# Projecting queries and keys in 64-row pairs, with the maxima steps spread one to a tile

## The chip, the cores and the metric

The kernel runs on one NeuronCore of a Trainium2 chip. The metric is the device time of one execution in microseconds (us): the median of several runs. A profiled execution gives the trace, from which single rows are read. The engines are PE (TensorE: matmuls, with PEld its weight loads), ACT (ScalarE), DVE (VectorE), POOL (GpSimd) and SP (SyncE, which here issues most DMAs).

## The reference

The result mixes an attention block and a Fourier block by a gate per row, for 2048 rows of width 640:

```
x = A_x                                    # (1, 2048, 640)
g = sigmoid((x * gate_w).sum(-1))
qkv = x @ wqkv                             # 32 heads of 20
p = softmax(q @ k.T * 20 ** -0.5)
a = (p @ v).reshape(1, 2048, 640) @ wo
b = Cr @ (x @ Wre.T) - Ci @ (x @ Wim.T)    # Cr, Ci: 2048 x 2048
out = g * a + (1 - g) * b
```

Inputs and output are float32. The weights wqkv and wo are large (scaled by 64), so the scores are large too and the softmax needs the maximum of every row.

## The kernel before

**Numbers as two parts.** A float32 factor is kept as two parts of the type fp32r: its rounded value and the rest. A product of two such factors takes three matmuls: first by first, first by second, second by first (`three`, L117 to L120). `split` (L110) makes the two parts: a copy by one engine (L112 or L114) and a subtraction by another (L115).

**Stages.** All instructions are put in order by hand, in program order for each engine; semaphores do the rest.

1. Load x and the first weights; project the queries and keys of the first column blocks and all values (up to about 107 us in the profile). `qk_tile(c, t)` (L301) projects column block `c` (128 columns of the queries or keys) for row block `t` (512 rows): 5 blocks of the inner dimension x 3 products = 15 matmuls of 128 x 128 weights on 512 columns, into one PSUM bank.
2. The stretch that the change touches, from about 107 to 256 us: the loop over `order` (eight column blocks, four row blocks each, 32 tiles) projects the rest of the queries and keys. Three things take turns on PE in it:
   - a projected tile, with `hid_done` above 0: ACT copies the bank to SBUF (L319), POOL splits the copy into two parts (L114 and L115), and SP stores both to DRAM (`stores`, `flush`, L299);
   - a feature tile (`hid_tile`, L352), the first step of the Fourier block. Its 15 products are issued as pairs: the 128 inner rows are cut into halves of 64 rows, and the two halves go into two banks of their own, `yp0` and `yp1` (L362). ACT copies one bank (L370), DVE adds the other (L371), SP stores the sum;
   - a maxima step (`s_step`, L188): for two heads, a matmul of 60 rows on 512 columns each (L170) into a bank, and for each bank a DVE maximum along its 512 columns (L172). The two heads lie in partitions 0 to 59 and 64 to 123. These are the row maxima that the attention needs; `LEAD` = 41 steps are to be done before the attention begins.
3. From about 256 us on: attention, with the remaining feature tiles and the sequence transform filled into PE's queue after a written pattern (`ORDER`), and at the end the output projection.

**Segments.** Ahead of every third projected tile (`m % 3 == 0`), ten times (`HEAD`), stands `segment` (L377). By `FILL[4] = (0, 8, 7, 0)` it issues four maxima steps in this order: step, step, 8 pairs of the feature tile, step, 7 pairs, step. A projected tile holds no step. One last step follows after the loop (`run_s(LEAD)`).

**Banks.** `bank()` (L124) hands out five PSUM banks in turn, `ps0` to `ps4`, to every user alike: projected tiles, maxima steps (two banks each), the transpose of the maxima (L204, once in this stretch, after step 33). Whoever gets a bank waits until its last reader is done. Three more banks are `av`, `yp0` and `yp1`.

**Other work in the stretch.** After the second tile of a column block the loaded weights are split by ACT and DVE: once the wide weights of a feature stage (L112 and L115, tile `wb`), otherwise 128 x 640 of the next column block (tile `part`).

Of the kernel before, what the change touches and what calls it, by code (L numbers as in the profile page):

```python
# [11 lines left out]
R = mybir.dt.float32r  # L12
AF = mybir.ActivationFunctionType
ALU = mybir.AluOpType
# [9 lines left out]
ND = D // P  # L24
# [15 lines left out]
LEAD = 41  # L40


FILL = {4: (0, 8, 7, 0)}
HEAD = 10


# [23 lines left out]
def f32(ap):  # L70
    return ap.bitcast(F32)
# [3 lines left out]
def mix_kernel(ctx: ExitStack, tc: tile.TileContext, xa, wqk, wb, cdft, wo, out):  # L75
    nc = tc.nc
    pe, act, dve, pool, sp = nc.tensor, nc.scalar, nc.vector, nc.gpsimd, nc.sync
# [32 lines left out]
    def split(dst1, dst2, src, e1, e2):  # L110
        if e1 is act:
            act.activation(dst1, src, AF.Copy)  # L112
        else:
            e1.tensor_copy(dst1, src)  # L114
        e2.tensor_tensor(dst2, src, f32(dst1), op=ALU.subtract)  # L115

    def three(ps, st1, st2, mv1, mv2, first, last):  # L117
        pe.matmul(ps, st1, mv1, start=first, stop=False)  # L118
        pe.matmul(ps, st1, mv2, start=False, stop=False)  # L119
        pe.matmul(ps, st2, mv1, start=False, stop=last)  # L120
# [3 lines left out]
    def bank():  # L124
        return ps_w.tile([P, 512], F32, name=f"ps{next(turn) % 5}")

    def pair_tile():
        return work.tile([P, 2, 512], F32, name="p", bufs=5)

    def raw_tile():  # L130
        return work.tile([P, 1024], F32, name="raw", bufs=3)
# [56 lines left out]
    def s_step(i):  # L188
        for fn in [s_mm(i, h) for h in range(2)]:
            fn()  # L190
        s_end(i)
# [4 lines left out]
    def new_y(z):  # L196
        yp[z] = ps_y.tile([P, 512], F32, name=f"yp{z}")
        return yp[z]
# [26 lines left out]
    def block(z, t):  # L225
        return proj.tile([P, ND * 512], R, name=f"x{z}{t}")

    xs = [[block(z, t).rearrange("p (d c) -> p d c", d=ND) for t in range(4)] for z in range(2)]
# [32 lines left out]
    def idle(n):  # L261
        ps = bank()
        for _ in range(n):
            pe.matmul(ps, zeros[:, :P], zeros, start=True, stop=True)

    wt = {}

    def load_wqk(c):
        raw = raw_tile()[:, : ND * P].rearrange("p (d c) -> p d c", d=ND)
        sp.dma_start(raw, wqk[c])  # L270

        def finish():
            w = part_tile().rearrange("p z c -> p (z c)")[:, : 2 * ND * P].rearrange("p (z d c) -> p z d c", z=2, d=ND)
            split(w[:, 0], w[:, 1], raw, act, dve)
            wt[c] = w

        return finish
# [17 lines left out]
    stores, halves, hid_done = [], [], 0  # L295

    def flush(keep=0):
        while len(stores) > keep:
            sp.dma_start(*stores.pop(0))  # L299

    def qk_tile(c, t):  # L301
        w = wt[c]
        ps = bank()
        x1, x2 = xs[0][t], xs[1][t]
        for d in range(ND):
            if (c, t) == (0, 0) and d > 0:
                if d == 1:
                    idle(3)
                pe.matmul(ps, w[:, 0, d], x1[:, d], start=False, stop=False)
                pe.matmul(ps, w[:, 1, d], x1[:, d], start=False, stop=False)  # L310
                pe.matmul(ps, w[:, 0, d], x2[:, d], start=False, stop=d == ND - 1)
            else:
                three(ps, w[:, 0, d], w[:, 1, d], x1[:, d], x2[:, d], d == 0, d == ND - 1)
        if hid_done:
            if not halves:
                raw = pair_tile()
                halves.extend((raw[:, 1], raw[:, 0]))
            raw = halves.pop()
            act.activation(raw, ps, AF.Copy)  # L319
        st = pair_tile()  # L320
        st1, st2 = st[:, 0].bitcast(R), st[:, 1].bitcast(R)
        if hid_done:
            split(st1, st2, raw, pool, pool)
        else:
            split(st1, st2, ps, act, dve)
        stores.append((qk_scr[:, t, c * P : (c + 1) * P].rearrange("z p c -> p z c"), st))
        flush(1 if hid_done else 2)

    def mm_b(j, s, ps, n):
        w = wt["b", j]  # L330
# [21 lines left out]
    def hid_tile(i, read_out):  # L352
        j, st = divmod(i, NS)
        hf, ri = divmod(j, 2)
        new_y(0), new_y(1)
        w = wt["b", 2 + j]
        t, cs = st // 4, slice(st % 4 * P, (st % 4 + 1) * P)
        for d in range(ND):
            for z, (xz, wz) in enumerate(((0, 0), (0, 1), (1, 0))):
                for h in range(2):  # L360
                    r = slice(64 * h, 64 * h + 64)
                    pe.matmul(yp[h][:, :HE], xs[xz][t][r, d, cs], w[r, wz, d, :HE],  # L362
                              start=d == 0 and z == 0, stop=d == ND - 1 and z == 2)
                if (d, z) != (ND - 1, 2):
                    yield
        a = raw_tile()[:, :HE]
        y0, y1 = yp[0][:, :HE], yp[1][:, :HE]

        def read():
            act.activation(a, y0, AF.Copy, scale=-1.0 if ri else 1.0)  # L370
            dve.tensor_tensor(a, a, y1, op=ALU.subtract if ri else ALU.add)  # L371

        read_out(read, (a_scr[ri, hf, st], a))
        yield


    def segment(i, steps):  # L377
        def read_out(read, args):
            read()
            stores.append(args)  # L380

        tile_ = hid_tile(i, read_out)
        for n in FILL[steps]:
            run_s(step + 1)
            for _ in range(n):
                next(tile_)

    step = 0

    def run_s(upto):  # L390
        nonlocal step
        while step < upto:
            s_step(step)
            step += 1
# [5 lines left out]
    for t in range(4):  # L400
        for c in (0, ND):
            qk_tile(c, t)
        if t == 0:
            fin()
        if t < 2:
            load_x(t + 2)
        if t == 3:
            fin = load_wb(1)
        for s in range(4 * t - 4, 4 * t, 2):
            if t:  # L410
                v_pair(0, s)
# [10 lines left out]
    def load_v(p):  # L422
        vts[p] = v_tile()
        sp.dma_start(vts[p], v_scr[p])
# [12 lines left out]
    for n, c in enumerate(order):  # L437
        for t in range(4):
            m = 4 * n + t
            if m % 3 == 0 and hid_done < HEAD:  # L440
                segment(hid_done, 4)
                hid_done += 1
            qk_tile(c, t)
            if m == 8:
                load_v(0)
            if t == 1:
                if n + 1 < len(order):
                    fin()
                if n + 2 < len(order):
                    fin = load_wqk(order[n + 2])  # L450
# [132 lines left out]
    st = {(th * HT + t, hf): 0 for th in range(2) for t in range(HT) for hf in range(2)}  # L583
# [197 lines left out]
    start = 4 * HID  # L781
# [5 lines left out]
    for u in range(UNITS):  # L787
        k, t = LONG[u // HT], u % HT
# [3 lines left out]
    for u in range(2 * len(PRE)):  # L792
        n = 2 if u >= 2 * len(PRE) - SLOW else 1
# [12 lines left out]
    for k, tt in enumerate(PRE):  # L806
        i = 4 * tiles[2 * k]
# [221 lines left out]
```

## Time and profile before

| | us |
|---|---|
| median of 3 runs | 1883.07 (1882.94 to 1885.08) |
| the profiled execution, its time | 1884.04 |
| the profiled execution, its span | 1882.3 |
| PE busy in the span | 1872.6 |
| DVE busy | 1448.1 |
| ACT busy | 1220.9 |
| POOL busy | 1070.4 |
| projected matmuls on 512 columns (L118, L119, L120), 107 to 256 us | 480 |
| maxima steps in the same stretch | 41 |
| feature tiles in the same stretch | 10 |

The span runs from the first to the last instruction; the time of a run also holds what lies around it. A row of the timeline has the start, the length, the engine, the line, the operation, what it writes and reads, the shapes and a count; in brackets stands how long the engine sat idle before, and what released it. Matmuls overlap, and their ends are modelled: how fast PE goes is read from the distances between starts, not from lengths. A pair of half-height matmuls starts nearly at once and counts as two.

### The profile page before, as it was taken

The numbers are of one execution on the slowest core, as the hardware profiler recorded it, in microseconds if no ns is written. First come the engines' busy times: TensorE is split into PE (matmuls) and PEld (weight loads), VectorE is DVE, ScalarE is ACT, GpSimd is POOL, SyncE is SP. The second block draws the span as 40 slices with busy tenths as digits, with TensorE's granted clock in tenths as the row PEclk, the third lists the DMA queues.
The fourth block names the chain that finished last, engine by engine and source line by source line (L and its number), as shares of the span: only waits on it lengthen the run. The fifth ranks groups of instructions, "written<-read, shape, count | busy, mean of one in ns | idle before, by whom it ended". The sixth has DMA issues, their size and how long they took to land. (4 is left out here: it accounts for less than half of the span.)

```text
span 1882.3 us, 44545 instructions
## 1 busy us (share of the span) xinstructions
PE 1872.6 (99%) x17453; PEld 1357.0 (72%) x17453; DVE 1448.1 (77%) x2410; ACT 1220.9 (65%) x2353; POOL 1070.4 (57%) x936
## 2 busy tenths in 40 slices
PE   9999999999999999999999999999999999999998
PEld 8988777777776777767677776777767676766666
DVE  4143468989898888888888888888888888889954
ACT  4221147777777766767676676766767676677785
POOL 1234421010045896566899899778789988634433
PEclk9999999999999999999999999999999999999999
DMA  7843341212425473537666576546475747342214
GB/s 232 179 136 137 137 142 48 78 60 64 117 69 182 148 230 127 162 123 186 196 186 223 173 248 190 167 130 189 159 233 196 221 144 197 117 116 63 62 44 151
DMA packets 174597, 280.51 MB, mean 149 GB/s; under 512 B 44095, under 2 KB 106687, under 8 KB 174387
## 3 DMA queue, kind: packets, MB, share of 16 engines
q1 hardware_dynamic: 173427, 275.69, 48.2%
q0 software_dynamic: 960, 1.97, 0.6%
q8 instruction: 137, 2.24, 0.5%
q14 instruction: 73, 0.60, 0.1%
HBM read 213.37 MB, written 63.52 MB: 147 GB/s over the span
## 5 line engine op out<-in xcount | busy, mean ns | idle before, releaser
L172 DVE TENSOR_REDUCE mx<-ps 128x1 f32<-128x512 f32 x2048 | 1295.5, 684 | 219.4 <-PE ps L170 201.7
L875 ACT ACTIVATE p<-ps 128x512 f32<-128x512 f32 x2048 | 1087.6, 599 | 430.1 <-PE ps L170 230.3
L170 PE MATMUL ps<-kst,qst 60*128 60x512 f32 x2048 | 775.7, 413 | 1.5 <-DVE mx L172 1.4
L873 PE MATMUL ps<-qst,kst 62*128 62x512 f32 x2048 | 703.9, 414 | 0.1
L613 PE MATMUL yp<-x,part 64*128 64x320 f32 x5376 | 644.9, 307 | 0.0
L613 PEld LDWEIGHTS yp<-x,part 64*128 64x128 f32 x5376 | 579.3, 186 | 7.5
L532 PE MATMUL av<-p,v 128*21 128x512 f32 x4096 | 492.1, 596 | 0.0
L873 PEld LDWEIGHTS ps<-qst,kst 62*128 62x128 f32 x2048 | 337.0, 184 | 201.0 <-DVE mx L172 182.2
L170 PEld LDWEIGHTS ps<-kst,qst 60*128 60x128 f32 x2048 | 368.2, 184 | 15.0 <-issue 3.8
L115 POOL TENSOR_TENSOR part<-raw,part 128x1024 fp32r<-128x1024 f32 (+1 forms) x129 | 290.6, 2252 | 10.3
L532 PEld LDWEIGHTS av<-p,v 128*21 128x21 f32 x4096 | 98.4, 100 | 227.0 <-issue 224.8
L362 PE MATMUL yp<-wb,x 64*128 64x320 f32 x1920 | 227.6, 307 | 0.3 <-ACT raw L370 0.2
L114 POOL CAST part<-raw 128x1024 fp32r<-128x1024 f32 (+1 forms) x129 | 127.3, 987 | 166.7 <-PE yp L613 145.3
L362 PEld LDWEIGHTS yp<-wb,x 64*128 64x128 f32 x1920 | 202.1, 186 | 5.1 <-DVE raw L371 0.7
L493 POOL TENSOR_TENSOR raw<-raw,raw 128x1024 f32<-128x1024 f32 x77 | 185.1, 2404 | 26.6 <-DMA raw<-in_cdft 26.3
L562 POOL TENSOR_TENSOR o<-o,rb 128x512 f32<-128x512 f32 x31 | 40.1, 1294 | 149.5 <-DMA rb<-r_scr 105.1
L684 PE MATMUL yp<-x,part 64*128 64x320 f32 x720 | 96.0, 310 | 0.0
L118 PE MATMUL ps<-x,part 128*128 128x512 f32 (+1 forms) x236 | 91.2, 386 | 0.3
L120 PE MATMUL ps<-x,part 128*128 128x512 f32 (+1 forms) x236 | 89.7, 380 | 0.0
L119 PE MATMUL ps<-x,part 128*128 128x512 f32 (+1 forms) x236 | 89.4, 379 | 0.0
L115 POOL TENSOR_TENSOR x<-araw,x 128x320 fp32r<-128x320 f32 x96 | 83.9, 874 | 7.7
L684 PEld LDWEIGHTS yp<-x,part 64*128 64x128 f32 x720 | 81.7, 186 | 2.9
(85 smaller groups left out, 1079.6 us busy)
## 6 DMA issues: line engine op xcount, KB each, us to landing
raw<-in_cdft SPq DMA_DIRECT2D x192, 512.0 KB
araw<-a_scr SPq DMA_DIRECT2D x176, 160.0 KB
qk_scr<-p SPq DMA_DIRECT2D x40, 512.0 KB
kst<-qk_scr SPq DMA_DIRECT2D x90, 160.0 KB
qst<-qk_scr SPq DMA_DIRECT2D x90, 160.0 KB
a_scr<-raw SPq DMA_DIRECT2D x64, 160.0 KB
yt<-y_scr SPq DMA_DIRECT2D x64, 160.0 KB
y_scr<-yt SPq DMA_DIRECT2D x64, 160.0 KB
```

The costliest lines, as they stand in the source:

```text
L114: e1.tensor_copy(dst1, src)
L115: e2.tensor_tensor(dst2, src, f32(dst1), op=ALU.subtract)
L118: pe.matmul(ps, st1, mv1, start=first, stop=False)
L170: pe.matmul(ps, q[b : b + KROWS, qt * P : (qt + 1) * P], k[b : b + KROWS, kc * 512 : (kc + 1) * 512], start=True, stop=True)
L172: return lambda: dve.tensor_reduce(mx[n][:, h, qt, kc : kc + 1], ps, axis=AX.X, op=ALU.max)
L362: pe.matmul(yp[h][:, :HE], xs[xz][t][r, d, cs], w[r, wz, d, :HE], start=d == 0 and z == 0, stop=d == ND - 1 and z == 2)
L493: pool.tensor_tensor(raws[0], raws[0], raws[1], op=ALU.add if PRODUCTS[n][0][1][0] > 0 else ALU.subtract)
L532: pe.matmul(av[32 * j : 32 * j + DH + 1, :], v[:, kt, h * (DH + 1) : (h + 1) * (DH + 1)], pp[qc][:, h, :], start=kt == 0, stop=kt == NS - 1)
L613: pe.matmul(yp[h][:, :HE], c[r, cz, cs], a[r, az], start=s == 0 and z == 0, stop=s == NS - 1 and z == 2)
L684: pe.matmul(yp[h][:, :HE], o[r, oz, d], wos[d, hf][r, wz], start=d == 0 and z == 0, stop=d == ND - 2 and z == 2)
L873: pe.matmul(pt, k[b : b + KROWS + 2, kt * P : (kt + 1) * P], q[b : b + KROWS + 2, qc * 512 : (qc + 1) * 512], start=True, stop=True)
L875: act.activation(pts[n, kt, qc][:, h], pt, AF.Exp, scale=float(DH) ** -0.5)
```

## The change

- In `qk_tile`, once `hid_done` is above 0 (all 32 tiles of the stretch), the 15 matmuls of 128 rows become 15 pairs of 64 rows (`qk_pairs`). The lower and the upper half of the inner rows go into two banks of the ring, taken together at the tile's start.
- ACT copies the first bank to SBUF as before; a new DVE instruction adds the second bank to the copy. POOL's split and the store are as before.
- `segment` and its `FILL` are gone. `tick` issues one maxima step after the seventh pair of every projected tile and every feature tile (`MARKS`), up to `LEAD`. The last of the 42 marks finds none left.
- The feature tile (`hid_first`) is issued at the same places as the segment was, with its add and store as before.
- The tiles of the first stage, before `hid_done`, are as they were.

```diff
-FILL = {4: (0, 8, 7, 0)}
+MARKS = (7,)
...
     def qk_tile(c, t):
+        if hid_done:
+            return qk_pairs(c, t)
...
-        if hid_done:
-            if not halves:
-                raw = pair_tile()
-                halves.extend((raw[:, 1], raw[:, 0]))
-            raw = halves.pop()
-            act.activation(raw, ps, AF.Copy)
         st = pair_tile()
-        st1, st2 = st[:, 0].bitcast(R), st[:, 1].bitcast(R)
-        if hid_done:
-            split(st1, st2, raw, pool, pool)
-        else:
-            split(st1, st2, ps, act, dve)
+        split(st[:, 0].bitcast(R), st[:, 1].bitcast(R), ps, act, dve)
+        store_qk(c, t, st, 2)
+
+    def store_qk(c, t, st, keep):
         stores.append((qk_scr[:, t, c * P : (c + 1) * P].rearrange("z p c -> p z c"), st))
-        flush(1 if hid_done else 2)
+        flush(keep)
+
+    def tick(pairs):
+        if pairs in MARKS:
+            run_s(min(step + 1, LEAD))
+
+    def qk_pairs(c, t):
+        w = wt[c]
+        ps = [bank(), bank()]
+        for d in range(ND):
+            for z, (wz, xz) in enumerate(((0, 0), (0, 1), (1, 0))):
+                for h in range(2):
+                    r = slice(64 * h, 64 * h + 64)
+                    pe.matmul(ps[h], w[r, wz, d], xs[xz][t][r, d], start=d == 0 and z == 0, stop=d == ND - 1 and z == 2)
+                tick(3 * d + z + 1)
+        if not halves:
+            raw = pair_tile()
+            halves.extend((raw[:, 1], raw[:, 0]))
+        raw = halves.pop()
+        act.activation(raw, ps[0], AF.Copy)
+        dve.tensor_tensor(raw, raw, ps[1], op=ALU.add)
+        st = pair_tile()
+        split(st[:, 0].bitcast(R), st[:, 1].bitcast(R), raw, pool, pool)
+        store_qk(c, t, st, 1)
...
-    def segment(i, steps):
+    def hid_first(i):
         def read_out(read, args):
             read()
             stores.append(args)
 
-        tile_ = hid_tile(i, read_out)
-        for n in FILL[steps]:
-            run_s(step + 1)
-            for _ in range(n):
-                next(tile_)
+        for pairs, _ in enumerate(hid_tile(i, read_out)):
+            tick(pairs + 1)
...
             if m % 3 == 0 and hid_done < HEAD:
-                segment(hid_done, 4)
+                hid_first(hid_done)
                 hid_done += 1
             qk_tile(c, t)
```

## Prediction

> **What bounds the kernel now.** I read the page first (engines, slices, clock), then the stage that the diff touches, by the view of busy time per stretch, by groups of lines, by waits and by the timeline.
>
> ```profile
> PE 1872.6 (99%) x17453; PEld 1357.0 (72%) x17453; DVE 1448.1 (77%) x2410; ACT 1220.9 (65%) x2353; POOL 1070.4 (57%) x936
> PEclk9999999999999999999999999999999999999999
> 107.00:256.00 149.00, 147.48 (x865) 119.31 (x863) 60.97 (x101) 28.70 (x51) 62.78 (x62) 1.00 0.38 135
> ```
>
> The columns of the last row are the stretch, its length, busy time of PE, PEld, DVE, ACT and POOL, then granted clock, DMA share and GB/s. This stretch holds the 32 query and key tiles, ten feature tiles and 41 maxima steps. TensorE is busy for 147.48 of 149.00 us at full clock; DVE (61), ACT (29) and POOL (63) have room. So the stage lasts as long as PE's queue, and what PE waits longer here the kernel lasts longer: no other engine has work that spans its end.
>
> One cycle of three projected tiles and a segment shows PE's prices:
>
> ```profile
> 149.68 0.39 PE L119 MATMUL ps<-x,part 128*128 128x512 f32 x1
> 149.91 0.40 PE L120 MATMUL ps<-x,part 128*128 128x512 f32 x1
> 150.23 0.72 PE L170 MATMUL ps<-kst,qst 60*128 60x512 f32 x4
> 150.80 1.34 PE L362 MATMUL yp<-wb,x 64*128 64x320 f32 x16
> 151.98 0.40 PE L170 MATMUL ps<-kst,qst 60*128 60x512 f32 x2
> 152.22 1.19 PE L362 MATMUL yp<-wb,x 64*128 64x320 f32 x14
> 153.25 0.40 PE L170 MATMUL ps<-kst,qst 60*128 60x512 f32 x2
> 153.58 0.50 PE L118 MATMUL ps<-x,part 128*128 128x512 f32 x1
> 153.92 0.39 PE L119 MATMUL ps<-x,part 128*128 128x512 f32 x1
> ...
> 163.77 0.40 PE L120 MATMUL ps<-x,part 128*128 128x512 f32 x1
> 164.09 0.30 PEld L170 LDWEIGHTS ps<-kst,qst 60*128 60x128 f32 x4 [0.36 <-issue]
> ...
> 164.20 0.60 ACT L319 ACTIVATE p<-ps 128x512 f32<-128x512 f32 x1 [2.76 <-PE ps L120]
> ```
>
> Matmuls overlap, so I take distances between starts. A full 128-row matmul: from 153.92 (the second of 45) to 163.77 (the last) are 43 steps, 0.229 each. A 64-row pair of 320 columns: (151.98 - 150.80) / 8 = 0.147. A maxima pair of 60 rows and 512 columns: 152.22 - 151.98 = 0.24. From full to 60 rows: 150.23 - 149.91 = 0.32, which is 0.09 over pace, and the two steps behind it take 0.57, 0.09 over twice 0.24; back again 0.33 and 0.34, 0.09 and 0.11 over. So a change of row mode costs PE 0.2 us.
>
> **What goes.** In before's stretch the mode changes 21 times (into and out of ten segments, and ahead of the last step). After, everything from the first feature tile on is in 60- or 64-row halves; one change at the start stays. 20 x 0.2 = 4.0 us go. (The transpose of the first unit's maxima changes it in both.)
>
> Two of the ten segments are longer than the others:
>
> ```profile
> 135.07:139.70 4.63, 3.91 (x39) 3.11 (x38) 3.27 (x6) 1.58 (x3) 2.46 (x2) 1.00 0.65 217
> 150.23:153.58 3.35, 3.35 (x39) 2.94 (x39) 2.82 (x5) 0.73 (x2) 1.90 (x2) 1.00 0.79 259
> ```
> ```profile
> 136.81 0.40 PE L170 MATMUL ps<-kst,qst 60*128 60x512 f32 x1
> 137.91 0.50 PE L170 MATMUL ps<-kst,qst 60*128 60x512 f32 x1 [0.70 <-DVE mx L172]
> 137.91 1.38 PE L362 MATMUL yp<-wb,x 64*128 64x320 f32 x13
> 139.06 0.39 PE L170 MATMUL ps<-kst,qst 60*128 60x512 f32 x1
> 139.14 0.30 PE L362 MATMUL yp<-wb,x 64*128 64x320 f32 x1
> 139.28 0.40 PE L170 MATMUL ps<-kst,qst 60*128 60x512 f32 x1
> ```
>
> There a weight split held DVE, four steps in one segment wanted eight banks out of a ring of five, and PE waited. Spread one per tile, the maxima come every 2.5 us or more for 1.4 us of DVE. Twice 1.28 us go: 2.6.
>
> **What comes: the second bank.** The ring of five is what I worked through. A tile now takes two banks (a, b), the step inside it two (c, d); the next tile takes the fifth, and then a again. Its second matmul therefore waits until ACT has copied a, the bank that the tile before has only just filled; PE works its queue in order, so everything behind it waits too. Before, the next tile needed one bank and the ring gave a free one.
>
> How long, counted from the start t of a tile's last matmul: ACT starts at t + 0.43 (163.77 to 164.20 above) and takes 0.60. Restart and wake-up:
>
> ```profile
> 82.46 0.16 ACT L345 ACTIVATE logit<-ps 128x1 f32<-128x1 f32 x1
> ...
> 82.67 0.19 PEld L118 LDWEIGHTS ps<-wb,x 128*128 128x128 f32 x1 [0.77 <-ACT logit L345]
> 82.68 0.42 PE L118 MATMUL ps<-wb,x 128*128 128x322 f32 x1 [0.51 <-ACT logit L345]
> ...
> 82.93 0.32 PE L119 MATMUL ps<-wb,x 128*128 128x322 f32 x1
> ```
>
> PE loads weights 0.05 after ACT's end (82.62 to 82.67), and the matmul behind comes 0.25 later where pace is 0.15: 0.10 for a load that nothing covered. The waiting matmul thus starts in effect at t + 0.43 + 0.60 + 0.05 + 0.10 = t + 1.18 instead of t + 0.23: 0.95 us lost. That is the first wait. Each later one is shorter, as the segment at 137.91 shows: when the waiting half starts, the next matmul of the other half starts with it, and from then on the halves run out of step (the last step's two at 139.06 and 139.28). Here the upper half then leads by one matmul, bank a is full 0.23 earlier, and the loss is 0.72.
>
> Where does it happen? At every passage from one projected tile to the next without a feature tile between: 31 passages less nine = 22. At the nine, the feature tile (15 x 0.147 + 0.24 = 2.4 us) covers copy and add. 0.95 + 21 x 0.72 = **16.1 us**.
>
> The added DVE sum of the second bank has its nearest row here, beside the copy's:
>
> ```profile
> L115 DVE TENSOR_TENSOR p<-ps,p 128x512 fp32r<-128x512 f32 x8 | 5.3, 687 | 17.7 <-ACT p L112 17.7
> L319 ACT ACTIVATE p<-ps 128x512 f32<-128x512 f32 x31 | 18.5, 598 | 91.1 <-PE ps L120 91.1
> L115 POOL TENSOR_TENSOR p<-p 128x512 fp32r<-128x512 f32 x31 | 43.6, 1407 | 2.5
> L114 POOL CAST p<-p 128x512 fp32r<-128x512 f32 x31 | 19.2, 618 | 85.6 <-ACT p L319 85.6
> ```
>
> It is 0.69 behind ACT's copy, frees bank b at t + 1.6, and b is wanted by the next tile's step, seven pairs in (t + 2.3): covered, 22 DVE us in all. Behind it queue POOL's cast and subtraction, 2.0 us in a tile of over 3.4, and SP's store: covered. Three small ones are not. The transpose takes one bank, so that once a tile wants b, not a: + 0.7. One split of wide weights (DVE, once) delays one sum past its feature tile: + 0.2. The last sum stands ahead of the attention's first maxima: + 0.2 (0 to 0.7).
>
> **Pairs against full matmuls.** 480 full ones become 480 pairs of 512 columns, which before doesn't show in a row. Nearest: the maxima pair's 0.24 from above (480 x 0.011 = + 5.3); at 320 columns pairs and full ones are equal:
>
> ```profile
> 106.04 0.31 PE L120 MATMUL ps<-wb,x 128*128 128x322 f32 x1
> ...
> 106.92 0.30 PE L120 MATMUL ps<-wb,x 128*128 128x322 f32 x1
> ```
>
> six steps, 0.147, like the pair's 0.147. From the other side: 320 to 512 columns is 0.147 to 0.229, 0.427 ns a column, 0.2187 for 512 if changing weights cost nothing (480 x -0.0103 = -4.9). I take 0.233, between the two nearest rows: + 1.9. The Trainium skill ("TensorE: Matmul & The Clock Gate", section "Wait — 56ns, not 53.3ns?") has 215.7 ns for a warm matmul of 512 columns; by it the pairs would save up to 6.4 us and the sum below would be + 4.2, but the full matmuls' 229 here don't reach it.
>
> **Sum.** - 4.0 - 2.6 + 16.1 + 0.7 + 0.2 + 0.2 + 1.9 = **+ 12.5 us**. Against the profiled execution (1884.04 us; span 1882.3) that is 1896.5; the median of the runs, 1883.07, is 1.0 lower: **1895.5**.
>
> **Rivals.**
> - *No lead* (0.11): the halves fall back into step after each wait. All 22 cost 0.95: + 17.3, 1900.4. Against it stand 139.06 and 139.28.
> - *The free half runs on* (0.05; the faster side): if PE lets the half that doesn't wait pass the waiting matmul, its lead grows with each wait, bank a is full four matmuls early, and the copy is done when it is wanted. It decides from a lead of about four (0.72 / 0.23 more than one). Then one wait stays, and with pairs at 0.229: 0.95 + 0.4 - 4.0 - 2.6 = - 5.3, 1877.8. Against it: between 136.81 and 137.91 one half waited and the other, which had work, started nothing. The Trainium skill (same page, Part 2, "Step-by-step") says that only weight loads are pulled ahead and matmuls stay in program order; the trace agrees.
> - *Pairs without a swap cost* (0.08): 0.2187 a pair, + 5.7, 1888.8. Against it the equal 0.147.
> - *The clock falls* (0.02): short waits at every tile could take the clock down; at half of it some 140 us of matmuls would take 140 more, near 2035. Against it: the 1.1 us wait at 136.81 left the clock at 1.00 (row of 135.07) and the pace at 0.147. The Trainium skill (same page, "A second HAM failure mode: psum-queue depth-cycling") tells of just such a case: small idles from cycling PSUM banks made the clock swing; no run here shows it.
>
> **Chances.** Forecast 0.74, with its own range of 1889 to 1902. A measurement of this kernel can tell about 0.2% (3.8 us) from no change. Faster 0.04 (the free half), same 0.05 (0.01 of it, 0.04 of cheap pairs), slower 0.91. The range runs from cheap pairs with the three small terms at nothing (5.7 - 1.1 = + 4.6, 1887.7) to no lead with pairs at 0.24 (17.3 + 3.4 = + 20.7, 1903.8, cut to 1903).
>
> **What would show it.** Of the changed kernel: an idle of about 0.7 ahead of the second matmul of most projected tiles, put down to the ACT copy, and none behind feature tiles; the two halves one matmul apart; no 0.32 between projected and feature tiles; pair pace 0.229 to 0.24; the stretch from the first feature tile to the attention 160 to 162 long instead of 149, the rest as long as before. I am wrong if that copy is not what ends PE's waits, or if the pairs' pace lies outside 0.219 to 0.24.

## The result, and the profile after

| | before, us | after, us |
|---|---|---|
| median | 1884.07 (4 runs, 1882.94 to 1885.11) | 1897.60 (4 runs, 1896.61 to 1897.85) |
| profiled execution's span | 1882.3 | 1895.6 |

The ratio after to before is 1.0074, with a 95% interval of 1.0061 to 1.0086: slower by 13.5 us, where 12.5 was forecast (1895.5 us, 1887.7 to 1903).

From the page of the changed kernel, the span, the busy time of each engine and the clock:

```profile
span 1895.6 us, 45562 instructions
...
PE 1874.5 (99%) x17933; PEld 1359.6 (72%) x17933; DVE 1473.5 (78%) x2442; ACT 1220.7 (64%) x2353; POOL 1070.5 (56%) x936
...
PEclk9999999999999999999999999999999999999999
```

The shares hardly differ from before's: PE's busy time grew by 2 us while the span grew by 13. Of DVE's 25 us more, 22 are the 32 sums (0.69 each); what they cost is seen below. The page doesn't show the loss; the stretch does. From the last value matmul to the first score matmul of the attention, by the view of busy time per stretch, first of before, then of after (length, busy PE, PEld, DVE, ACT, POOL, then clock, DMA share and GB/s):

```profile
106.92:256.24 149.32, 147.80 (x867) 119.55 (x866) 60.97 (x101) 28.94 (x52) 62.78 (x62) 1.00 0.38 135
```
```profile
106.20:267.30 161.10, 150.04 (x1348) 122.84 (x1347) 86.43 (x134) 28.73 (x52) 63.17 (x62) 1.00 0.36 126
```

11.8 us of the span's 13.3 arose here: PE was without a matmul for 1.5 us before and for 11.1 after. The other 1.5 are a sum of three: the stage ahead was 0.7 shorter in this one execution, what follows up to the last matmul 0.7 longer, and 1.6 lie behind the last matmul. Who ended PE's idle time, by the view of waits of after (engine, line, what for, total, times, longest):

```profile
PEld ps L335 <- ACT p L341: 20.3, 22, 1.2
...
PE ps L335 <- ACT p L341: 10.8, 22, 0.7
...
PEld ps L335 <- DVE p L342: 0.5, 1, 0.5
```

22 times the projected matmuls waited for ACT's copy, and once for the DVE sum. (PEld's sum is larger than PE's since the loads stop first, while a matmul still runs.) One such passage, and what follows, in the timeline of after:

```profile
115.46 2.01 PE L335 MATMUL ps<-x,part 64*128 64x512 f32 x16
...
117.28 0.60 ACT L341 ACTIVATE p<-ps 128x512 f32<-128x512 f32 x1 [3.83 <-PE ps L335]
...
117.91 0.69 DVE L342 TENSOR_TENSOR p<-p,ps 128x512 f32<-128x512 f32 x1 [1.17 <-ACT p L341]
...
117.94 1.88 PE L335 MATMUL ps<-x,part 64*128 64x512 f32 x13 [0.46 <-ACT p L341]
...
119.21 0.41 PEld L170 LDWEIGHTS ps<-kst,qst 60*128 60x128 f32 x2
...
119.44 0.61 PE L170 MATMUL ps<-kst,qst 60*128 60x512 f32 x2
```

ACT's copy ends at 117.88 and PE goes on at 117.94. The sum runs beside PE. The two maxima matmuls take 0.61 from the first's start to the second's end, 0.22 more than one of them: the halves run one matmul apart (the lead), as forecast. By the starts in the trace, the copy begins 0.45 after the last matmul into its own bank and 0.20 after the last into the other.

### The profile page after: what moved, and what is told of

The parts are those of the page before. It is cut to its first block, busy times and chain, and to the rows that moved or that the text cites. A ratio compares the mean times of both kernels' runs of the same rounds, so it can differ in the third digit from the quotient of the medians.

```text
span 1895.6 us, 45562 instructions
## 1 busy us (share of the span) xinstructions
PE 1874.5 (99%) x17933; PEld 1359.6 (72%) x17933; DVE 1473.5 (78%) x2442; ACT 1220.7 (64%) x2353; POOL 1070.5 (56%) x936
## 5 line engine op out<-in xcount | busy, mean ns | idle before, releaser
L890 ACT ACTIVATE p<-ps 128x512 f32<-128x512 f32 x2048 | 1087.6, 599 | 432.0 <-PE ps L170 226.2
L170 PE MATMUL ps<-kst,qst 60*128 60x512 f32 x2048 | 784.0, 412 | 0.1
L170 PEld LDWEIGHTS ps<-kst,qst 60*128 60x128 f32 x2048 | 375.0, 184 | 10.4 <-ACT p L890 0.5
L335 PE MATMUL ps<-x,part 64*128 64x512 f32 x960 | 128.5, 395 | 11.1 <-ACT p L341 10.8
L335 PEld LDWEIGHTS ps<-x,part 64*128 64x128 f32 x960 | 98.1, 185 | 36.1 <-ACT p L341 20.3
L341 ACT ACTIVATE p<-ps 128x512 f32<-128x512 f32 x32 | 19.1, 597 | 114.0 <-PE ps L335 101.0
```

Source lines behind the costliest of these rows:

```text
L170: pe.matmul(ps, q[b : b + KROWS, qt * P : (qt + 1) * P], k[b : b + KROWS, kc * 512 : (kc + 1) * 512], start=True, stop=True)
L335: pe.matmul(ps[h], w[r, wz, d], xs[xz][t][r, d], start=d == 0 and z == 0, stop=d == ND - 1 and z == 2)
L890: act.activation(pts[n, kt, qc][:, h], pt, AF.Exp, scale=float(DH) ** -0.5)
```

## The experiments

The theory: at a passage from one projected tile to the next, the second matmul waits for the bank that ACT is still copying. Rivals: the sums and their traffic, the pairs themselves, the spreading of the steps, or the clock. Each ratio is to the kernel before on the same chip; its median there was 1883.10 for the steps in other banks, the short sum and the early step, and 1882.95 for the other four.

**The tiles in other banks.** Every second projected tile behind a feature tile goes into `yp0` and `yp1`:

```diff
+    place = [0]
...
-        ps = [bank(), bank()]
+        ps = [new_y(0), new_y(1)] if place[0] % 2 else [bank(), bank()]
+        place[0] += 1
...
+        place[0] = 0     # at the end of hid_first
```

> Every second projected tile behind a feature tile takes the two feature banks (idle then) instead of two banks of the ring of five; nothing else changes. Theory (PE waits for the ACT copy of the bank that the tile before has just filled): the waits of 0.73 us at tile-to-tile passages go, all but the one passage left inside the ring in the last group; 22 x 0.75 = 16 us less than the changed kernel, 1881 us, some 3 us under the kernel before. Rival (the loss comes from the added DVE sums, their traffic beside POOL, or from the pairs themselves): 1896 to 1898 us, as the changed kernel.

Measured: 1879.28 us (11 runs), ratio 0.9981 (0.9972 to 0.999). This is faster than both kernels, though than the one before by 0.2% only. (The last group alternates too, so that no passage is left inside the ring; the expectation was wrong in that.) Its stretch and PE's waits in it:

```profile
106.47:250.25 143.78, 143.19 (x1347) 127.98 (x1347) 86.07 (x134) 28.70 (x51) 63.16 (x62) 1.00 0.40 141
```
```profile
PEld ps L337 <- DVE p L344: 0.8, 1, 0.8
PE ps L337 <- DVE p L344: 0.6, 1, 0.6
PEld ps L204 <- issue: 0.4, 1, 0.4
```

The same matmuls, copies, sums and steps in 143.8 instead of 161.1 us: 17.3 us go with the 22 waits, and DVE is as busy as before (86). Neither the sums nor the pairs carry the loss. One wait is left, behind the split of the wide weights.

**The steps in other banks.** The projected tiles stay in the ring, and the step inside them leaves it:

```diff
+    inside = [False]
...
-        ps = bank()
+        ps = new_y(h) if inside[0] else bank()    # in s_mm
...
+                inside[0] = True     # in qk_pairs
                 tick(3 * d + z + 1)
+                inside[0] = False
```

> Another way to the same end: the projected tiles keep two banks of the ring, but the maxima step inside a projected tile uses the two feature banks. So the ring gives the next tile two banks that have long been free. Theory (a clash in the ring): the waits at tile-to-tile passages go as they did with the tiles in the feature banks, 1879 to 1881 us. Rival (it was the feature banks themselves that helped the projected tiles): 1896 to 1898 us.

Measured: 1882.06 us (11 runs), ratio 0.9993 (0.9984 to 1.0002). No wait for ACT's copy is left here either, so it was the order of the ring and not which banks. PE's waits in the stretch are two, of one kind:

```profile
PE yp L383 <- DVE mx L173: 2.0, 2, 1.8
```

With this the run misses the expected 1879 to 1881. The timeline behind the split of the wide weights:

```profile
118.14 3.31 DVE L115 TENSOR_TENSOR wb<-raw,wb 128x966 fp32r<-128x966 f32 x2 [0.21 <-ACT wb L112]
...
121.36 1.27 DVE L173 TENSOR_REDUCE mx<-yp 128x1 f32<-128x512 f32 x2
...
122.09 0.41 PE L383 MATMUL yp<-wb,x 64*128 64x320 f32 x1 [1.83 <-DVE mx L173]
...
122.69 1.72 PE L383 MATMUL yp<-wb,x 64*128 64x320 f32 x12 [0.19 <-DVE mx L173]
...
124.63 2.15 PE L383 MATMUL yp<-wb,x 64*128 64x320 f32 x15
```

The feature tile now waits for the maxima, and they stand behind the split on DVE. What this wait did to the clock is told below.

**The wait made longer.** The two banks of a tile swapped between the halves:

```diff
-        ps = [bank(), bank()]
+        ps = [bank(), bank()][::-1]
```

> The changed kernel with the two banks of a projected tile swapped between the halves: the next tile's first matmul now wants the bank that the DVE sum reads, which comes 0.74 us behind the ACT copy. Theory: at 22 passages the wait grows from 0.75 to about 1.7 us (no half gets ahead, so 0.23 of it is the lost lead), + 20 us, and about 0.4 at nine feature tiles: 1917 to 1921 us, with the waits put down to the DVE sum. Rival (the wait for the bank isn't what sets the time): 1897 us.

Measured: 1920.31 us (4 runs), ratio 1.0196 (1.0182 to 1.0209). PE's waits:

```profile
PEld ps L335 <- DVE p L342: 37.5, 22, 1.9
...
PE ps L335 <- DVE p L342: 28.2, 22, 1.5
...
PEld ps L170 <- DVE p L342: 4.7, 9, 0.6
```

Same work, other bank: the 22 waits are now for the sum (at the transpose for the copy first), and the nine small ones in the feature tiles are there. The time grew with the wait, as the theory asks.

**The sum made short.** One column of 512 is summed; the rest of the second bank is left out:

```diff
-        dve.tensor_tensor(raw, raw, ps[1], op=ALU.add)
+        dve.tensor_tensor(raw[:, :1], raw[:, :1], ps[1][:, :1], op=ALU.add)
```

> The changed kernel with the DVE sum cut to one column of 512; the other 511 columns of the upper halves' sums are left out. Theory: the sum of 0.69 us lies beside PE's work at all but three places (transpose, wide weights, start of the attention), so 1 us at most is won: 1896 to 1897.5 us, with the 22 waits unchanged and still put down to the ACT copy. Rival (DVE's or POOL's extra work carries the loss): 1881 to 1890 us.

Measured: 1895.09 us (5 runs), ratio 1.0064 (1.0051 to 1.0076). The waits for the copy stand as they were:

```profile
PEld ps L335 <- ACT p L341: 20.3, 22, 1.2
...
PE ps L335 <- ACT p L341: 10.8, 22, 0.7
```

So the waits carry the loss and not the sums. By the ratios 32 sums cost about 2 us, twice what I allowed, but the two intervals overlap. In the traces, 0.5 lies at the transpose and 0.8 at the attention's start (from its first score matmul to its 401st value matmul 163.5 instead of 164.3 us; one trace each, and the run with spreading alone, which has no sum, took 164.1).

**The step earlier.** After the second pair of a projected tile instead of the seventh:

```diff
-                tick(3 * d + z + 1)
+                tick(3 * d + z + 6)
```

> The changed kernel with the step after the second pair of a projected tile instead of the seventh (feature tiles as they were). Theory with a lead of one matmul: the step then wants the tile before's second bank 0.28 us before the DVE sum has freed it, and as both halves restart together there, the lead is lost and the next passage costs 0.95 instead of 0.72: 22 x 0.5 = 11 us more, 1908 us. Without a lead that can be lost: 22 x 0.28 = 6 us more, 1904 us. Rival (the sum is always covered): 1897 us.

Measured: 1905.44 us (4 runs), ratio 1.012 (1.0104 to 1.0135), 8 us above the changed kernel. One passage in its timeline:

```profile
118.31 0.60 ACT L341 ACTIVATE p<-ps 128x512 f32<-128x512 f32 x1 [4.30 <-PE ps L335]
...
118.94 0.69 DVE L342 TENSOR_TENSOR p<-p,ps 128x512 f32<-128x512 f32 x1 [2.33 <-ACT p L341]
...
118.96 0.73 PE L335 MATMUL ps<-x,part 64*128 64x512 f32 x3 [0.46 <-ACT p L341]
119.68 0.19 PEld L170 LDWEIGHTS ps<-kst,qst 60*128 60x128 f32 x2 [0.43 <-DVE p L342]
119.69 0.50 PE L170 MATMUL ps<-kst,qst 60*128 60x512 f32 x2
```

The sum ends at 119.63, and the step's two matmuls start together at 119.69 (0.50 long both, so at once): 20 of the 22 passages have this second wait, of about 0.26. From there the halves run in step. By the distances between starts most passages then cost 0.94 to 1.02, against 0.74 to 0.81 in the changed kernel, over all 22 together 21.7 against 18.0 us. The mechanism is that of the forecast with a lead; its price of 0.5 was too high, 0.4 is what came out (20 x 0.26 + 3.7 = 8.9 us).

**Spreading alone.** Full matmuls into one bank, and so no sum, with a step after the seventh product of every tile:

```diff
-        ps = [bank(), bank()]
+        ps = bank()
...
-                for h in range(2):
-                    r = slice(64 * h, 64 * h + 64)
-                    pe.matmul(ps[h], w[r, wz, d], xs[xz][t][r, d], ...)
+                pe.matmul(ps, w[:, wz, d], xs[xz][t][:, d], ...)
                 tick(3 * d + z + 1)
...
-        act.activation(raw, ps[0], AF.Copy)
-        dve.tensor_tensor(raw, raw, ps[1], op=ALU.add)
+        act.activation(raw, ps, AF.Copy)
```

> One part alone: maxima steps spread one to a tile after the seventh product, projected tiles as before in full 128-row matmuls and one bank. Theory: no bank waits, the two waits of the long segments go (2.6 us), but each of 31 steps inside a full tile costs two changes of row mode of 0.2 us, 12.4 us: 1884 + 9.8 = 1894 us, with distances of 0.32 and 0.33 around each step. Rival (a change of row mode costs nothing that isn't also in a step's own price, and the pairs bring the whole loss): 1881 to 1884 us.

Measured: 1892.60 us (5 runs), ratio 1.005 (1.0038 to 1.0063). In its timeline, PE alone:

```profile
122.40 0.40 PE L170 MATMUL ps<-kst,qst 60*128 60x512 f32 x2
122.64 1.34 PE L377 MATMUL yp<-wb,x 64*128 64x320 f32 x16
123.91 1.88 PE L333 MATMUL ps<-x,part 128*128 128x512 f32 x7
125.72 0.49 PE L170 MATMUL ps<-kst,qst 60*128 60x512 f32 x2
```

Seven full matmuls take 125.72 - 123.91 = 1.81 instead of 7 x 0.229 = 1.60 up to the step's start. A cycle of three tiles lasts 15.07, against 13.86 before: 1.21 for six more changes of row mode, 0.20 each. A maxima step is cheap only beside work in the same row mode.

**Pairs alone.** Tiles in pairs, and four steps to a segment as before:

```diff
-                tick(3 * d + z + 1)
...
-        for pairs, _ in enumerate(hid_tile(i, read_out)):
-            tick(pairs + 1)
+        tile_ = hid_tile(i, read_out)
+        for n in (0, 8, 7, 0):
+            run_s(step + 1)
+            for _ in range(n):
+                next(tile_)
```

> The other part alone: projected tiles in pairs with two banks and the DVE sum, maxima steps four to a segment as before. Theory (banks): without the step between them, neighbouring tiles find a bank that has long been free, so no waits at tile-to-tile passages; but in each segment the second step wants the bank that ACT is just copying (0.7 us), and the tile behind wants banks whose maxima DVE has not read (about 1.1 us): ten times 1.8, less 0.7 in the first, 17 us, against 6.6 saved: 1894 us, 1891 to 1897. Rival (each pair tile costs by itself, through the DVE sum or its pace): waits at tile-to-tile passages stay, 1897 us or more.

Measured: 1892.10 us (5 runs), ratio 1.0046 (1.0033 to 1.006). The waits of PE:

```profile
PEld ps L335 <- DVE mx L172: 6.7, 18, 0.4
PEld ps L170 <- ACT p L340: 6.5, 10, 0.7
...
PE ps L170 <- ACT p L340: 2.2, 9, 0.3
PEld ps L170 <- DVE mx L172: 1.8, 3, 0.7
```

No projected matmul waits for a copy any more, so a passage without a step in it finds a free bank. The step in the segment waits for the copy, and the next tile for the maxima. Each part of the change alone costs 9 to 10 us, through different things; neither holds the wait that the two make together.

## Why the prediction was right

- **The waits** (forecast 16.1, and 0.7 at the transpose): 18.0 us by the distances between starts. The first, without a lead, cost 0.91 (forecast 0.95), those with the full lead 0.74 to 0.81 (0.72), one where the halves were only 0.09 apart 0.87, the one at the transpose 1.73 (0.72 + 0.7; the transpose also put the halves back in step, which the forecast left out). It is the lower half that leads, not the upper as the prediction says: the bank that ACT copies is the lower half's. The sum frees its bank at t + 1.5 with the lead and at t + 1.7 without, where the prediction says t + 1.6 for both; it is covered either way. That they set the time is shown in both directions: taken away in two ways they bring the kernel to 1879 and 1882 us, made longer they take it to 1920.
- **What goes** (4.0 and 2.6): the run with spreading alone confirms 0.20 a change of mode. In the changed kernel, a cycle of three tiles and a feature tile is 15.04 long: 13.86 - 0.4 + 0.74 + 0.79 = 14.99.
- **The pairs** (+ 1.9, between - 4.9 and + 5.3): nothing. A pair of 512 columns goes at the pace of the full matmul. From the first projected tile in the timeline of after:

```profile
108.97 1.82 PE L335 MATMUL ps<-x,part 64*128 64x512 f32 x14
...
110.59 0.43 PE L170 MATMUL ps<-kst,qst 60*128 60x512 f32 x2
```

  (110.59 - 108.97) / 7 = 0.231, and 0.229 over longer pieces. The maxima pair's 0.24 was the wrong neighbour; equality at 320 columns was the right one. The 215.7 ns of the Trainium skill ("TensorE: Matmul & The Clock Gate", section "Wait — 56ns, not 53.3ns?") are reached by neither. This term was mis-sized by 1.9 us.
- **The small ones** (0.2 at the wide weights, 0.2 at the attention): 0.1 and 0.8.

The errors were of either sign, 1.9 too much for the pairs, 1.7 too little for waits, transpose and attention together, so the sum is nearer than its terms by luck. Within the stretch: 18.0 - 4.0 - 2.6 = 11.4, where 11.8 was measured. The 1.6 us behind the last matmul are no term of the forecast. That tail was 5.0 us in the traces of before and of spreading alone, and 5.7 to 6.8 in those of the seven kernels with pairs; why is open.

- **Rivals.** *No lead* is refuted by the changed kernel, and the run with the early step shows what its loss costs. *The free half runs on* is refuted: the lead never went above one matmul (0.25 us at most between the halves' last starts), though 22 waits offered the chance. *Pairs without a swap cost* fell with 0.229. *The clock* stayed at 1.00 in the stretch through all 22 short waits.

## What to carry to other kernels

Count the banks that are asked for from one tile to the next, not those in use: with four requests a tile on a ring of five, each tile's second request meets the bank that is being emptied, however idle the reader is. A request that is moved or added changes who meets whom for every user of the ring, and a way round may cost nothing (here two banks that lay idle between feature tiles). A change that saves at the edges of a group, 6.6 us here, is first weighed against what it adds at every passage inside it.

## What the runs showed of the hardware

In one trace the clock fell behind a wait. With the steps in the feature banks, PE's wait for the maxima (1.83 us without a matmul, then 0.19) was followed by this, in the view of busy time per stretch:

```profile
118.00:122.00 4.00, 2.26 (x20) 1.56 (x16) 3.87 (x4) 1.33 (x3) 2.67 (x2) 1.00 0.53 173
122.00:126.00 4.00, 3.71 (x27) 3.49 (x29) 2.36 (x5) 0.00 (x0) 1.88 (x2) 0.63 0.27 100
126.00:130.00 4.00, 4.00 (x38) 4.00 (x38) 1.94 (x4) 0.44 (x1) 0.00 (x0) 0.95 0.46 172
```

The granted clock was 0.63 over four microseconds and was back behind 126. In between, the 15 feature matmuls from 124.63 took 2.15 us where 16 took 1.34 before; by the starts in the trace a pair of 320 columns took 0.266 instead of 0.147. That is part of why this kernel stayed 2.8 us above the one with the tiles in the feature banks: the cycle with the wait lasts 15.59 us against 13.59 there, the next one, with the low clock, 15.61 against 14.38, and from the third on both have 13.49. The Trainium skill ("TensorE: Matmul & The Clock Gate", Part 1) puts the fall to half clock behind an idle window of about 3.4 us. Here it came once behind an idle time of 1.83 us.

The length of the idle time alone doesn't decide it. The 22 waits of under a microsecond in the changed kernel and the 22 of up to 1.5 us with the two banks swapped left the clock at 1.00 over the whole stretch. So did one of 1.95 us in the first stage of the run with the early step: its full matmuls behind it, from 10.40 us on, are 0.23 apart, as at full clock. What else decides was not tried.
